# The last load of wo split in two, and the second half of K*e moved behind the next head's row maximum, in a one-core forward and backward decode kernel

## The chip, the cores and the metric

The kernel runs on one core of one Trainium2 chip. Its time is the device time of one execution in microseconds (us). The core has TensorE (PE; its weight loads are listed apart as PEld), VectorE (DVE), ScalarE (ACT) and GpSimd (POOL); SyncE (SP) issues most loads and computes nothing. Each engine works through its own list of instructions in order; what one makes for another is handed over by a semaphore, and an instruction that waits holds up all that stands behind it on its engine. Sixteen DMA engines move data between HBM and the on-chip memory.

## The reference

Both outputs and all gradients of a block with one query per batch element are computed (B = 2, H = 32 heads, 4096 cached keys, head size 128, D = 640, Dff = 1728):

```python
q = layernorm(x) @ wq                       # per head: [B, H, 1, 128]
scores = einsum("bhqd,bhkd->bhqk", q, k_cache) * 128 ** -0.5
p = softmax(scores);  o = einsum("bhqk,bhkd->bhqd", p, v_cache)
h  = x + o @ wo
h2 = h + relu(layernorm(h) @ w1) @ w2
out, vjp = jax.vjp(f, x, k_cache, v_cache, wq, wo, w1, w2);  return out, *vjp(grad_out)
```

The caches hold 64 heads (batch element and head) of 4096 x 128 numbers, 1 MiB each for K and for V. The gradients for K and V are as large again.

## The kernel before

The 64 heads pass the core twice. The **first pass** (`p1_iter`, L459 to L584) reads K and V of each head, forms the scores s = K q, e = exp(s - max), and three sums over the keys: V^T e, V^T (K*e) (a 128 x 128 matrix) and the column sums of K*e. The **second pass** (`p2_iter`, `p2_tail`) reads V once more (tile W), forms dP = V go and writes gK and gV. Between them stands the middle of each batch element (`middle_gen`): attention output times wo, layer norm, MLP forward and backward, and then the products of wo with the gradient, row by row (`go_group`), which the second pass of a head waits for. These rows, and those of w1 and w2 before, are dot products on DVE of 640 numbers (`ttr`, L656; called "row products" below); a counter `slot` says how many of them may be issued in each step of an iteration.

**One iteration of the first pass** is a software pipeline over three heads: head i is scored, K*e is formed for head i-1, and the sums over V are made for head i-2. It runs in steps k = 0 to 7, each ended by a `yield`, at which the loop at L1219 slips in steps of the second pass, the middle's work and the issue of loads. Per iteration:

- k0: PE transposes two quarters of K (T, L433), copied to SBUF by ACT (L438).
- k1: PE spreads the row maximum of head i-1 over all partitions (MX, L512), DVE reduces it to nb (L514); PE does the first 8 of 32 matmuls of V^T(K*e) for head i-2 (`m_part`, L467).
- k2: ACT makes ep = exp (L521); third transposed quarter; scores of quarter 0 (`pair_matvec`, L446).
- k3: `m_part(2)`; DVE forms the first half of K*e for head i-1 (`pk_half(0)`, L474); scores of quarter 1; last transposed quarter, copied by DVE up to i = 32 (L436) and by ACT afterwards.
- k4: `u_part` (column sums), `m_part(3)`, scores of quarter 2, `m_part(4)`.
- k5: second half of K*e (`pk_half(1)`), and K's buffer is given back; `m_part(5)`, `m_part(6)`; at its end `a_heads` (four heads of the attention output times wo, 20 matmuls at L603, added up by DVE at L605).
- k6: `m_part(7)`, scores of quarter 3, and DVE's row maximum rmax (L568), which the next iteration's MX waits for.
- k7: V's buffer is given back.

K*e has three buffers (`pk`, L481), so that its second half for one head goes where the first half for the head before was, which PE must have read (`u_part`, `m_part(3)`).

**Loads.** K, V, W and w2 share 13 tiles of 1 MiB (`ld`). All loads are issued by SP in one fixed order (`queue`, L1107 to L1123); a load waits until the tile that it goes to was given back and read, and those behind it wait too. In iteration i the next K and V are issued as soon as `pk_half(1)` and `m_part(7)` have let go of theirs. V of heads 26 to 31 stays for the second pass. wo comes in four quarters of 1280 KB, placed in the list at i = 10, 15, 29 and 33, and w1 at 35 (`W_AT`).

**Stages.** Iterations 0 to 33 are the first batch element alone, with w2's row products on DVE in iterations 12 to 29. Iterations 34 to 40 carry the first middle (w1's 15 row products, then wo's). From iteration 41 on (`P2_AT`) one head of the second pass runs beside every two iterations: in odd iterations PE also transposes W, in even ones DVE forms most of gK and gV (L830, written to HBM from POOL's queue). After iteration 65 the second pass runs alone. "Iteration 34" and the like mean i in `p1_iter(i)` below; its end is dated by its row maximum at L568.

Of the kernel before, what the change touches and what calls it, by code (L numbers as in the profile page):

```python
# [15 lines left out]
def kernel(  # L16
# [38 lines left out]
    OG = 4  # L55
# [285 lines left out]
    def pair_rows(dst, src, hs, bs):  # L341
# [6 lines left out]
        for c in range(2):  # L348
            rows = slice(64 * c, 64 * c + 64)
            for par in range(2):  # L350
                nc.vector.tensor_copy(out=dst[rows, bs, hs, par, c].rearrange("p b h -> p h b"), in_=t[rows, par, :, :])

    def load_weights(k):
        if k < 4:
            hs = slice(k * H // 4, (k + 1) * H // 4)
            nc.sync.dma_start(out=wo_t[:, hs, :], in_=wo_r[:, hs, :])
        elif k == 4:
            nc.sync.dma_start(out=w1_t[:], in_=B_w1.rearrange("(c p) f -> p c f", p=128))

    FP = 6  # L360
# [64 lines left out]
    def pair_transpose(nat, g, dve=False, busy=0):  # L425


        t_ps = pst([128, GT // 2, 128], FP32, "tps", "t_ps")
        warm(t_ps[:].rearrange("p j k -> p (j k)"), nat, g, busy)
        natf = nat[:].bitcast(FP32)  # L430
        for j in range(GT // 2):
            cc = (g * GT) // 2 + j
            nc.tensor.transpose(t_ps[:, j, :], natf[:, 2 * cc:2 * cc + 2, :].rearrange("p c k -> p (c k)"), ident_f[:])  # L433
        t_sb = mats.tile([128, GT // 2, 128], FP32, tag="XT", bufs=4, name="t_sb")
        if dve:
            nc.vector.tensor_copy(out=t_sb[:], in_=t_ps[:])  # L436
        else:
            nc.scalar.copy(out=t_sb[:], in_=t_ps[:])  # L438
        return t_sb

    def pair_matvec(dst, t_sb, g, vecs):
        v = t_sb[:].bitcast(BF16).rearrange("p j (k two) -> p j k two", two=2)
        for j in range(GT // 2):
            sc = g * GT + 2 * j
            for par in range(2):
                nc.tensor.matmul(dst[:, sc:sc + 2], lhsT=v[:, j, :, par], rhs=vecs[:, par, :],  # L446
                                 start=(par == 0), stop=(par == 1))
# [11 lines left out]
    def p1_iter(i, dve_group, busy):  # L459
# [5 lines left out]
        def m_part(k):  # L465
            for sc in range(4 * k, 4 * k + 4):
                nc.tensor.matmul(r["m"][:, 0:129], lhsT=r["V"][:, sc, :],  # L467
                                 rhs=r["pk"][sc // HALF][:, sc % HALF, 0:129],
                                 start=(sc == 0), stop=(sc == NSC - 1))

        def pk_half(k):

            sl = slice(k * HALF, (k + 1) * HALF)
            nc.vector.tensor_tensor(  # L474
                out=p["pk"][k][:, :, 0:128].rearrange("p s (a two) -> p s a two", two=2),
                in0=p["K"][:, sl, :].rearrange("p s (a two) -> p s a two", two=2),
                in1=p["ep"][:, sl, None, :].to_broadcast([128, HALF, 64, 2]), op=ALU.mult)
# [51 lines left out]
            c["s"] = c["bank"][:, 0:NSC]  # L529
            pair_matvec(c["s"], c.pop("KT0"), 0, q)  # L530
        yield
        if r is not None:
            m_part(2)
        if p is not None:
            pk_half(0)
        if c is not None:
            pair_matvec(c["s"], c.pop("KT1"), 1, q)
            c["KT3"] = pair_transpose(c["K"], 3, dve_group)
        yield
        if r is not None:  # L540
            u_part()
            m_part(3)
        if c is not None:
            pair_matvec(c["s"], c.pop("KT2"), 2, q)
        if r is not None:
            m_part(4)
        if p is not None and hp % OG == OG - 1:

            totp = p["bank"][:, 256:256 + OG]
# [2 lines left out]
        if p is not None:  # L552
            pk_tile(1)
            if hp % OG == OG - 1:
                nc.vector.reciprocal(out=rt[:, bp, hp + 1 - OG:hp + 1], in_=totp)
            (nc.gpsimd if i < P2_AT else nc.vector).tensor_copy(out=P_bf[:, p_slot[(bp, hp)], :], in_=ep[:, :, 0])
            pk_half(1)
            give(p["K"], "g" if i == P2_AT else None)
        if r is not None:
            m_part(5)  # L560
            m_part(6)
        yield
        if r is not None:
            m_part(7)
        if c is not None:
            pair_matvec(c["s"], c.pop("KT3"), 3, q)
            rmax = small.tile([128, 1], BF16, tag="rmax", bufs=2, name="rmax")
            nc.vector.reduce_max(out=rmax[:], in_=c["s"], axis=AX.X)  # L568
            c["rmax"] = rmax
        yield  # L570
        if r is not None:
            br, hr = pairs[i - 2]
# [35 lines left out]
    def a_heads(i):  # L608

        if a_next[0] < o_next[0]:  # L610
            a_group()
        if o_next[0] < NP1 // OG and i >= o_next[0] * OG + OG + 2:
            b, g = divmod(o_next[0], H // OG)
            if b > 0 or i >= O_AT[g * OG * 4 // H]:
                o_group()

    def u_out(b, u4):
# [41 lines left out]
    slot = [99]  # L659
# [445 lines left out]


    queue = []  # L1107
    W_AT = (10, 15, 29, 33, 35)
    O_AT = (14, 19, 30, 32)
    W2_AT = (8, 13, 18)  # L1110
    for n, (ii, jj) in enumerate(plan):
        if ii is not None:
# [45 lines left out]
    for n, (i, j) in enumerate(plan):  # L1158
        all_go = all(("go", B - 1, h) in done for h in range(H))
        if i is None and plan[n - 1][0] is not None:  # L1160
            pkp.release()
            big1 = tc.alloc_tile_pool(name="big1", bufs=1)
            for _ in range(2):
                more_home("ld", big1)
            share(ld=KEPT[1] + 4, g=5)
        if all_go and not late[0]:
            wop.release()
            big3 = tc.alloc_tile_pool(name="big3", bufs=1, side="right")
            for tag in ("ld", "g", "g", "q", "q", "q"):
                more_home(tag, big3)  # L1170
        late[0] = all_go
        more = int(late[0])
        if fin is not None and not bg2 and not bg3:
            share(ld=8 + 3 * more, g=7 + 3 * more)
        elif fin is not None and j >= H:
            held = sum(bh in kept for bh in turns[j + 1:])
            share(ld=5 + held + more, g=5 + 2 * more, f=3, q=2 + 3 * more)
        while g2 is not None:
            p2_step()
        open_tail = [k for k in S2 if "T3" in S2[k]]  # L1180
        if j is not None:
            if j < NP1:
                bg_until(("go", *turns[j]))
            g2 = p2_iter(j, i is None and j < H) if j < NP1 else p2_tail(NP1 - 1)
        elif open_tail:
            g2 = p2_tail(open_tail[0])
        if i is None and ("w1", 1) in done and fin is None:
            wts.release()
            fin = tc.alloc_tile_pool(name="fin", bufs=1)
            big2 = tc.alloc_tile_pool(name="big2", bufs=1)  # L1190
            more_home("f", big2)
            banks.update(sps=[2, 3], o=[4, 5, 6])
            bg2.append(("fin", fin_gen(fin)))
            bg3.append(("gx", gx_gen(fin)))
        if i == 12:
            bg.append(("ga", ga_gen()))
        if i == H + 2:
            banks["bc"].insert(0, banks["sps"].pop(0))
        elif i == P2_AT:
            banks["bc"].remove(7)  # L1200
            banks["sps"].insert(0, banks["bc"][0])
            banks["bc"] = [7]
        rate = RATES[0 if i is not None and i <= H + 1 else 1 if j is None and i < P2_AT else
                     2 if i is not None else 3 if j <= H else 4]
        if i is None:
            spread[0] = 2
            at_k[0] = 1
            k = 0
            while g2 is not None:
                p2_step()  # L1210
                pump()
                slot[0] = int(k in ((1, 3, 5) if j <= H else (1, 4)))
                k += 1
                bg_step(0, rate)
                bg_step(1, RATE2 * (0.4 if spreading[0] else 1.0))
                bg_step(2, RATE3)
            continue
        at = LIGHT if j is None else HEAVY_TAIL if open_tail else HEAVY
        for k, _ in enumerate(p1_iter(i, i < H + 1, 0)):  # L1219
            for _ in range(at.get(k, 0)):  # L1220
                if g2 is not None:
                    p2_step()
            if k == 5:
                a_heads(i)
            pump()

            spread[0] = 1 if i < P2_AT else 2
            at_k[0] = k
            if i >= P2_AT:
                slot[0] = int(k == 6 or (k == 1 and j is None))  # L1230
            elif i > H + 1:
                slot[0] = {1: 2, 3: 1, 4: 1, 6: 1}.get(k, 0)
            else:
                slot[0] = int(k in (1, 6))
            bg_step(0, rate)
            bg_step(1, 0.0)
        if i is not None and i in (H + 1, NP1 + 1):
            bg.append((f"m{i // H - 1}", middle_gen(i // H - 1)))
# [41 lines left out]
```

## Time and profile before

Three timed executions took 897.49, 898.05 and 899.12 us (median 898.05). The profiled execution took 896.79 us, of which the span of the core's instructions, which all views of the trace cover, is 895.0 us.

| what | profile before |
|---|---|
| PE, DVE, ACT, POOL busy | 745.7, 686.9, 482.9, 197.3 us of 895.0 |
| moved by DMA | 361.84 MB, mean 404 GB/s |
| half of K*e on DVE (L474) | 128 x 1221 ns |
| row product (L656), with its read of the sum | 816 + 81 ns |
| half of gK or gV on DVE (L830) | 1223 and 1143 ns |
| row maximum (L568), nb (L514) on DVE | 193 and 290 ns |
| last quarter's copy on DVE (L436) | 680 ns |
| SP waiting for K*e (L474) before a load | 124.7 us in 20 waits |
| SP waiting for PE's transposes (L433) | 257.7 us in 47 waits |

Times are counted from the span's start. DMA share is the busy share of the 16 DMA engines (1.0 is all of them, and records can overlap to slightly more). "PEclk" is the clock that PE was granted, as a share of the full one. A number in brackets in a timeline is the idle time of the engine before an instruction, with what ended it.

### The profile page before, as it was taken

Reading aid. Unit: us, or ns where it says so; the run is one execution under the profiler, and the core shown is the slowest. Engines: PE = TensorE matmul, PEld = TensorE weight load, DVE = VectorE, ACT = ScalarE, POOL = GpSimd, SP = SyncE. Lnnn points to the kernel's source line nnn. Section 1 sums busy time; section 2 is a strip of 40 time slices with the busy share of each in tenths; the row PEclk is TensorE's granted clock in tenths of the full one; section 3 lists DMA queues with packets and bytes.
Section 4 is the critical chain, followed back from the end, with each engine's and each line's share of the span. In section 5 each row is a group of like instructions: output and inputs, shape, how many; then the busy total and the mean of one; then the engine's idle time right before and its main releaser. Section 6 shows DMA issues by size and latency. Waiting matters only on the chain.

```text
span 895.0 us, 24702 instructions
## 1 busy us (share of the span) xinstructions
PE 745.7 (83%) x10145; PEld 622.3 (70%) x10145; DVE 686.9 (77%) x1283; ACT 482.9 (54%) x1236; POOL 197.3 (22%) x347
## 2 busy tenths in 40 slices
PE   4999899999998999797967786778797897978593
PEld 4887788888887888686857675566666665665452
DVE  2666788866888897686768896679986579998854
ACT  1344344443555655464535777776665765657462
POOL 1344444442310000000011241122221111111211
PEclk9999999998999999799885555555755755555555
DMA  9999999999989999999999999999999999999996
GB/s 379 419 412 402 411 407 419 409 412 411 358 300 365 423 422 424 423 421 424 401 398 381 418 418 415 390 419 391 416 420 404 426 424 425 424 424 426 423 411 277
DMA packets 56288, 361.84 MB, mean 404 GB/s; under 512 B 5680, under 2 KB 11888, under 8 KB 15472
## 3 DMA queue, kind: packets, MB, share of 16 engines
q1 hardware_dynamic: 34520, 211.13, 58.2%
q0 software_dynamic: 18432, 134.23, 36.1%
q10 hardware_dynamic: 3224, 14.92, 4.1%
q8 instruction: 80, 1.31, 0.6%
q14 instruction: 32, 0.26, 0.1%
HBM read 211.11 MB, written 149.13 MB: 403 GB/s over the span
## 4 chain that ended last, share of the span: by engine, by line
PE 37%; DMA 26%; DVE 21%; issue 7%; ACT 7%; SPq 0%; POOL 0%; ACTq 0%; POOLq 0%; DVEq 0%
PE t_ps L433 15%; DMA Vt<-in_A_v_cache_dram 11%; DMA out_dram<-gK 10%; PE m_ps L467 8%; DVE rows L656 5%; DVE gK L830 5%; DVE gV L830 5%; DMA out_dram<-gV 3%; DVE pk L474 3%; PE s_ps L446 3%; ACT gV L897 3%; PE u_ps L496 2%; PE o_ps L948 2%; PE dp_ps L446 2%; ACT t_sb L438 2%
## 5 line engine op out<-in xcount | busy, mean ns | idle before, releaser
L438 ACT COPY t_sb<-t_ps 128x512 f32<-128x512 f32 x479 | 271.8, 587 | 203.4 <-PE t_ps L433 200.4
L446 PEld LDWEIGHTS <-t_sb 128*128 128x128 bf16 x4096 | 180.8, 103 | 61.4 <-ACT t_sb L438 30.0
L433 PE MATMUL t_ps<-ident_f,Wt 128*128 128x128 f32 x832 | 202.5, 396 | 0.8 <-ACT t_sb L438 0.8
L474 DVE TENSOR_TENSOR pk<-Kt,ep 128x2048 bf16<-128x2048 bf16 x128 | 156.2, 1221 | 43.6 <-PE m_ps L467 20.1
L467 PE MATMUL m_ps<-pk,Vt 128*128 128x129 bf16 x2048 | 173.6, 223 | 15.2 <-DMA Vt<-in_A_v_cache_dram 14.7
L830 DVE TENSOR_TENSOR gK<-rb,gsp 128x2048 bf16<-128x2048 bf16 x128 | 153.0, 1223 | 13.7 <-DMA out_dram<-gV 12.1
L433 PEld LDWEIGHTS t_ps<-ident_f,Wt 128*128 128x128 f32 x832 | 141.6, 206 | 30.7 <-issue 22.3
L433 PE MATMUL t_ps<-ident_f,Kt 128*128 128x128 f32 x1024 | 154.2, 285 | 4.2 <-DMA Kt<-in_A_k_cache_dram 4.1
L467 PEld LDWEIGHTS <-Vt 128*128 128x128 bf16 x2048 | 125.4, 99 | 46.1 <-issue 28.7
L830 DVE TENSOR_TENSOR gV<-rb,pp 128x2048 bf16<-128x2048 bf16 (+1 forms) x128 | 143.3, 1143 | 12.3 <-DMA out_dram<-gK 9.8
L484 POOL COPY pk<-ep 128x16 bf16<-128x16 bf16 x80 | 85.2, 1067 | 152.7 <-ACT ep L521 72.4
L433 PEld LDWEIGHTS t_ps<-ident_f,Kt 128*128 128x128 f32 x1024 | 113.5, 145 | 5.1 <-PE s_ps L446 2.7
L446 PE MATMUL dp_ps<-gom,t_sb 128*128 128x2 bf16 x2048 | 96.4, 168 | 19.9 <-ACT t_sb L438 19.5
L898 POOL DMA_DIRECT2D out_dram<-gV x64 | 34.2, 534 | 314.2 <-DVE nb L514 114.2
L446 PE MATMUL s_ps<-gom,t_sb 128*128 128x2 bf16 x2048 | 87.5, 164 | 1.3 <-DVE t_sb L436 1.3
L849 POOL DMA_DIRECT2D out_dram<-gK x64 | 34.0, 532 | 210.4 <-DVE gK L830 164.0
L580 ACT CAST MT<-m_ps 128x128 bf16<-128x128 f32 x64 | 17.1, 267 | 104.9 <-PE m_ps L467 104.7
L954 ACT CAST ot<-o_ps 128x512 bf16<-128x512 f32 (+3 forms) x152 | 67.5, 491 | 3.1 <-PE o_ps L948 1.9
L656 DVE CUSTOM_DVE_ANT_0 rows<-wo_t,rows 128x640 bf16<-128x640 bf16 x64 | 52.4, 819 | 0.2
L841 DVE SCALAR_TENSOR_TENSOR gsp<-dp_ps,negdot,P_bf 128x64 bf16<-128x64 f32 x64 | 17.8, 279 | 42.5 <-PE dp_ps L446 42.4
L870 ACT ACTIVATE rb<-dp_ps,rt 128x256 bf16<-128x256 f32 x64 | 30.3, 473 | 36.9 <-PE dp_ps L865 35.7
L656 DVE CUSTOM_DVE_ANT_0 rows<-wqs,gqr 128x1024 bf16<-128x1024 bf16 x40 | 48.7, 1219 | 0.2
(194 smaller groups left out, 758.8 us busy)
## 6 DMA issues: line engine op xcount, KB each, us to landing
Kt<-in_A_k_cache_dram SPq DMA_DIRECT2D x64, 1024.0 KB, 16.9
Vt<-in_A_v_cache_dram SPq DMA_DIRECT2D x64, 1024.0 KB, 18.1
out_dram<-gV POOLq DMA_DIRECT2D x64, 1024.0 KB, 12.1
out_dram<-gK POOLq DMA_DIRECT2D x64, 1024.0 KB, 13.0
Wt<-in_A_v_cache_dram SPq DMA_DIRECT2D x52, 1024.0 KB, 11.7
out_dram<-ot ACTq DMA_DIRECT2D x6, 960.0 KB, 6.6
wq_t<-in_A_wq_dram SPq DMA_DIRECT2D x5, 1024.0 KB, 9.8
wo_t<-in_A_wo_dram SPq DMA_DIRECT2D x4, 1280.0 KB
```

The costliest lines, as they stand in the source:

```text
L433: nc.tensor.transpose(t_ps[:, j, :], natf[:, 2 * cc:2 * cc + 2, :].rearrange("p c k -> p (c k)"), ident_f[:])
L438: nc.scalar.copy(out=t_sb[:], in_=t_ps[:])
L446: nc.tensor.matmul(dst[:, sc:sc + 2], lhsT=v[:, j, :, par], rhs=vecs[:, par, :], start=(par == 0), stop=(par == 1))
L467: nc.tensor.matmul(r["m"][:, 0:129], lhsT=r["V"][:, sc, :], rhs=r["pk"][sc // HALF][:, sc % HALF, 0:129], start=(sc == 0), stop=(sc == NSC ...
L474: nc.vector.tensor_tensor(out=p["pk"][k][:, :, 0:128].rearrange("p s (a two) -> p s a two", two=2), in0=p["K"][:, sl, :].rearrange("p s (a ...
L484: nc.gpsimd.tensor_copy(out=col, in_=e)
L656: nc.vector.tensor_tensor_reduce(out=junk[0:kc, 0:width], in0=in0, in1=in1, scale=1.0, scalar=0.0, op0=ALU.mult, op1=ALU.add, accum_out=acc)
L830: nc.vector.tensor_tensor(out=pairs_view(dst[:, sl, :]), in0=row.rearrange("p (a two) -> p a two", two=2)[:, None, :, :].to_broadcast([128 ...
L849: nc.gpsimd.dma_start(out=natural(out_2, bp, hp), in_=gK[:])
L870: nc.scalar.activation(out=rb[:], in_=bank[:, 128:384], func=ACT.Copy, scale=rt[:, b, h:h + 1])
L898: nc.gpsimd.dma_start(out=natural(out_3, b, h), in_=gV[:])
L954: nc.scalar.copy(out=ot[0:P, k, n0:n0 + nn], in_=o_ps[0:P, 0:nn])
```

## The change

wo's last quarter is loaded as two parts of four heads, the second one iteration later, in front of w1's load. On PE, `m_part(2)` moves behind the scores of quarter 1, `m_part(3)` and `m_part(4)` ahead of `u_part`, and `m_part(7)` behind the scores of quarter 3. On DVE, `pk_half(1)` moves from step 5 to step 6, behind the row maximum of head i; K's buffer is given back there too. In iterations 34 to 40 the row products' slots move from steps 1, 3, 4, 6 (2, 1, 1, 1) to steps 1, 3, 4 (2, 2, 1). The order of ACT's and POOL's instructions is the same as before.

```diff
+    WO_PARTS = (0, H // 4, H // 2, 3 * H // 4, H - OG, H)
+
     def load_weights(k):
-        if k < 4:
-            hs = slice(k * H // 4, (k + 1) * H // 4)
+        if k < len(WO_PARTS) - 1:
+            hs = slice(WO_PARTS[k], WO_PARTS[k + 1])
             nc.sync.dma_start(out=wo_t[:, hs, :], in_=wo_r[:, hs, :])
-        elif k == 4:
+        else:
             nc.sync.dma_start(out=w1_t[:], in_=B_w1.rearrange("(c p) f -> p c f", p=128))
...
         yield
-        if r is not None:
-            m_part(2)
         if p is not None:
             pk_half(0)
         if c is not None:
             pair_matvec(c["s"], c.pop("KT1"), 1, q)
+        if r is not None:
+            m_part(2)
+        if c is not None:
             c["KT3"] = pair_transpose(c["K"], 3, dve_group)
         yield
         if r is not None:
+            m_part(3)
+            m_part(4)
             u_part()
-            m_part(3)
         if c is not None:
             pair_matvec(c["s"], c.pop("KT2"), 2, q)
-        if r is not None:
-            m_part(4)
...
             (nc.gpsimd if i < P2_AT else nc.vector).tensor_copy(out=P_bf[:, p_slot[(bp, hp)], :], in_=ep[:, :, 0])
-            pk_half(1)
-            give(p["K"], "g" if i == P2_AT else None)
         if r is not None:
             m_part(5)
             m_part(6)
         yield
-        if r is not None:
-            m_part(7)
         if c is not None:
             pair_matvec(c["s"], c.pop("KT3"), 3, q)
...
             c["rmax"] = rmax
+        if p is not None:
+            pk_half(1)
+            give(p["K"], "g" if i == P2_AT else None)
+        if r is not None:
+            m_part(7)
         yield
...
-            if b > 0 or i >= O_AT[g * OG * 4 // H]:
+            if b > 0 or i >= O_AT[g]:
                 o_group()
...
-    W_AT = (10, 15, 29, 33, 35)
-    O_AT = (14, 19, 30, 32)
+    W_AT = (10, 15, 29, 33, 34, 35)
+    O_AT = (14, 14, 19, 19, 30, 30, 32, 33)
...
-                slot[0] = {1: 2, 3: 1, 4: 1, 6: 1}.get(k, 0)
+                slot[0] = {1: 2, 3: 2, 4: 1}.get(k, 0)
```

As the lists of the two programs show, DVE in iterations 34 to 47 gets this order (pk is a half of K*e, ttr a row product, gkv a half of gK or gV, the rest small operations or named above):

```
36 before  small nb pk ttr ttr rt pk rmax
   after   pk small nb pk ttr ttr ttr rt rmax
37 before  ttr nb ttr ttr pk ttr ttr pk rmax
   after   pk nb ttr ttr pk ttr ttr ttr rmax
39 before  ttr nb ttr ttr small pk small pk small rmax
   after   pk nb ttr ttr small pk small rmax
40 before  nb ttr ttr small pk small pk rmax
   after   pk nb ttr ttr small pk small rmax
46 before  ttr gkv nb gsp ttr pk gkv Pbf pk small rmax
   after   pk ttr gkv nb gsp ttr pk gkv Pbf small rmax
47 before  gkv ttr nb pk Pbf pk gkv small rmax
   after   pk gkv ttr nb pk Pbf gkv small rmax
```

On PE the 20 matmuls of L603 for heads 28 to 31 stand where they stood, in iteration 34 ahead of MX and of the first `m_part`; their first weight load now waits for the second part of wo's last quarter.

## The prediction

> **What bounds the kernel now.** I read the page's slices first, then the stages by windows, then the waits of SP, and last the timelines of PE and DVE where a stage is not limited by DMA.
>
> ```profile
> PE   4999899999998999797967786778797897978593
> PEclk9999999998999999799885555555755755555555
> DMA  9999999999989999999999999999999999999996
> GB/s 379 419 412 402 411 407 419 409 412 411 358 300 365 423 422 424 423 421 424 401 398 381 418 418 415 390 419 391 416 420 404 426 424 425 424 424 426 423 411 277
> ```
>
> A slice is 22.4 us. The DMA engines are full nearly everywhere, at 402 to 419 GB/s while only reads run and about 423 when writes are mixed in; slices 10 to 12 stand out with 358, 300 and 365 GB/s. The stages:
>
> ```profile
> 0.00:224.00 224.00, 203.55 (x3494) 179.42 (x3495) 155.53 (x328) 86.09 (x252) 84.89 (x122) 0.98 1.01 408
> 224.00:252.00 28.00, 25.57 (x461) 22.34 (x459) 24.31 (x64) 13.79 (x39) 7.99 (x13) 1.00 0.92 358
> 252.00:282.00 30.00, 28.29 (x484) 25.12 (x483) 24.19 (x57) 18.28 (x49) 3.08 (x7) 1.00 0.83 300
> 282.00:343.00 61.00, 56.12 (x973) 49.78 (x971) 52.58 (x106) 36.41 (x100) 5.22 (x12) 1.00 1.01 423
> 432.00:464.00 32.00, 27.88 (x479) 24.36 (x477) 26.18 (x49) 18.07 (x50) 4.63 (x9) 1.00 0.99 389
> ```
>
> The columns are length, busy PE, PEld, DVE, ACT, POOL, clock, DMA share, GB/s. Up to 224 us DMA is full (1.01): no engine's order can shorten that stage, except through when it ends. From 224 to 282 us DMA waits for buffers: against 423 GB/s, 28 x (1 - 358/423) + 30 x (1 - 300/423) = 4.3 + 8.7 = 13.0 us are lost there. This hole is what the change can win or enlarge. It ends where the last loads that DMA idles for are issued:
>
> ```profile
> 280.24 0.33 SPq L454 DMA_DIRECT2D Vt<-in_A_v_cache_dram  x1
> 280.97 0.33 SPq L454 DMA_DIRECT2D Kt<-in_A_k_cache_dram  x1
> 281.91 0.33 SPq L454 DMA_DIRECT2D Vt<-in_A_v_cache_dram  x1
> ```
>
> Afterwards the queue never runs dry until 432 us, so what is lost or won up to these three lines is what the end shows, plus 432 to 464 us (389 GB/s).
>
> **The entry into the hole: wo's split.**
>
> ```profile
> 208.90 1.06 PE L433 MATMUL t_ps<-ident_f,Kt 128*128 128x128 f32 x8 [0.71 <-DMA Kt<-in_A_k_cache_dram]
> 209.80 0.64 PE L603 MATMUL a_ps<-OFc,wo_t 128*128 128x1 bf16 x20
> 210.31 0.22 PE L512 MATMUL s_ps<-neg_ident,rmax 128*128 128x128 bf16 x1
> 211.29 1.05 PE L467 MATMUL m_ps<-pk,Vt 128*128 128x129 bf16 x8 [0.77 <-DMA Vt<-in_A_v_cache_dram]
> ```
>
> In iteration 34 PE waits 0.71 us for K of head 34 and 0.77 us for V of head 32. Half a quarter of wo is 0.655 MB, at 411 GB/s 1.6 us: with only the first half ahead of them both land 1.6 us earlier, and both waits go. But the second half of wo, now last of the same bytes, lands when V did, at 211.2, and the 20 matmuls at L603 need it ahead of MX and of the first eight `m_part` matmuls. So these start at 211.2 + 0.5 (from 209.80 to 210.31) + 0.1 = 211.9 instead of 211.29. I take **+0.6 us**; the bounds are -1.6 (all of the earlier landing kept) and +0.6.
>
> **The middle, iterations 34 to 40.** The sums of DVE's work are the same per iteration, only pk changes sides of rmax.
> - 35 and 36: before, rmax at 219.09 is followed at once by small operations of the layer norm and nb starts at 220.08. Now pk (1.22) stands ahead of them; nb and the norm's result come about 1.5 us later. PE had spare time there (DVE idled 1.44 us before the rmax of 225.93), so I let +0.6 reach rmax 35, and +0.1 rmax 36. Bounds 0 and +1.5.
> - 34 and 35: `m_part(7)` leaves the way to rmax: 4 matmuls, 0.24 us each time (one such group starts at 222.55 and what follows it at 222.79). I take -0.3 of -0.48, since part of it falls where DVE sets the pace.
> - 37: DVE is full in 230 to 248 us; a pk (1.15 from start to start) stands in for a row product (0.87): **+0.3**.
> - 39: one row product of w1's last five (0.61 + 0.08) has moved to 36: **-0.6**.
> - 40: before, DVE idles 1.36 us for nb at 253.34; pk fits in: **-1.15**.
>
> With the split: 0.6 + 0.7 - 0.3 + 0.3 - 0.6 - 1.15 = **-0.45** at the end of iteration 40.
>
> **Beside the second pass.** An odd and the next even iteration:
>
> ```profile
> 289.73 0.18 DVE L568 TENSOR_REDUCE rmax<-s_ps 128x1 bf16<-128x32 f32 x1
> 291.71 0.28 DVE L514 TENSOR_REDUCE nb<-s_ps 128x1 f32<-128x128 f32 x1
> 293.21 0.66 PE L433 MATMUL t_ps<-ident_f,Vt 128*128 128x128 f32 x4 [0.41 <-ACT t_sb L438]
> 294.97 1.22 DVE L474 TENSOR_TENSOR pk<-Kt,ep 128x2048 bf16<-128x2048 bf16 x1 [1.19 <-PE m_ps L467]
> 297.57 0.19 DVE L568 TENSOR_REDUCE rmax<-s_ps 128x1 bf16<-128x32 f32 x1 [0.24 <-PE s_ps L446]
> 303.05 1.21 DVE L474 TENSOR_TENSOR pk<-Kt,ep 128x2048 bf16<-128x2048 bf16 x1
> 304.45 0.19 DVE L568 TENSOR_REDUCE rmax<-s_ps 128x1 bf16<-128x32 f32 x1
> ```
>
> From the even rmax to nb DVE is full (2.0 us); from nb over ACT's exp and copies to PE's transposes, on which PE waits 0.41 us, PE sets the pace up to the odd rmax (5.86); from there DVE is full to the next even rmax (6.88). The pair takes 14.72. The odd pk at 294.97 lies in a stretch where DVE idles anyway; moved behind the odd rmax it enters the DVE-bound even half, which hands its own pk on to the next odd one, ahead of nb. So the first piece grows by 1.15 to 1.25, the second shrinks by 0.24 (`m_part(7)`), the third keeps its work: **+1.0 us per pair**. For 41 to 44 that is +2.0; in 43 and 44 some small operations of `go_group` (0.75, 0.5 and a 0.87 row product) shift one iteration on, out of the PE-bound 43, for which I take -1.5: **+0.5**, bounds -1.0 and +2.0. From 282 to 432 us the same +1.0 is hidden by the full DMA; the cover is thin only at first.
>
> **Buffers.** K's tile is now free 1.35 us (0.1 + 1.22) after rmax. It was free at rmax in even iterations, and 1.9 us ahead of it in 43 (280.2 against 282.09). In program order the load of 280.24 now takes W's tile, released by PE at 280.95, the next K's, at 282.1 + 1.35 = 283.4. The three issues move by about +0.7, +2.5 and +1.5; I take **+1.5**, bounds 0 (the queue covers it) and +2.5.
>
> **432 to 464 us** holds one and a half pairs; DMA is nearly full, so I take half of +1.5: **+0.7**, bounds 0 and +1.5.
>
> **The first 224 us: 0.** Covered by DMA. Were DMA not the bound, the loop over nb, exp, pk, copy and rmax would lose a pk (5.22 to about 4.9 where no row product runs, PE then being the bound: 33 x 0.3 = 10 us won), while with two row products per iteration it would grow, since nothing covers the wait for the last scores any more (by some 0.4). SP's order of loads is not moved past anything but the second part of wo; it is one more issue, 0.4 us on a queue that issues 165.
>
> **Sum:** -0.45 + 0.5 + 1.5 + 0.7 = +2.25, say +2.2: span 897.2. The profiled execution was 1.8 us longer than its span and 1.26 us under the median, so against the median: 898.05 + 2.2 = **900.2 us**.
>
> **Rivals.**
>
> 1. *The clock stays full in iteration 34, and the earlier rmax pays: faster.* PE's clock falls behind a poorly filled stretch:
>
> ```profile
> 207.83:211.25 3.42, 1.98 (x41) 1.76 (x37) 1.93 (x10) 1.70 (x6) 0.08 (x1) 1.00 1.00 411
> 211.25:218.07 6.82, 6.78 (x69) 5.87 (x70) 3.17 (x11) 1.27 (x4) 0.76 (x2) 0.50 1.01 410
> ```
>
> 1.98 of 3.42 us busy (0.58), then 6.8 us at half clock, which cost about 3.4 us of PE work. A first pass that comes later to iteration 34 (row products ahead of nb in 13 to 28) or stalls that fall into two stretches would avoid it: -3.4. With the buffers' term at 0 as well: 2.2 - 3.4 - 1.5 = -2.7, **895.3 us**. Against it: wo's second part makes one wait of over 2 us out of two short ones. Chance 0.33, for both signs hang on 0.58 or a little more.
>
> The Trainium skill, TensorE: Matmul & The Clock Gate, "What's actually happening", says that the clock falls after at least one idle window of about 3.4 us; by that rule a wait of 2 us would not lower it, and the sum would be this rival's first step, 2.2 - 3.4 = -1.2. The trace does not agree: 0.58 busy was enough here, so I go by the trace.
>
> 2. *Nothing to be seen.* If the queue covers the later buffers and the end of the first pass, -0.45 + 0.5 are left: **898.1 us**. For it: 423 GB/s from 282 us on. Against it: the three issues above end an idle DMA. Chance 0.20.
>
> 3. *Slower by much more.* If the +1.0 is not hidden in the ten pairs from 43 to 64: 2.2 - 0.7 + 10 - 0.5 = +11, **909 us**. Against it: DMA at 1.01 from 282 to 432 us. Chance 0.09.
>
> **How the numbers follow.** The forecast has 0.38. Two executions differ by 0.2% (1.8 us) without a cause, so that is what I call no change. Faster 0.33 (rival 1), same 0.20 (rival 2), slower 0.47 (forecast and rival 3). The gaining bounds together are -1.6 - 3.4 - 0.3 - 0.6 - 1.15 = -7 (891), the losing ones 0.6 + 1.5 + 0.3 + 2.0 + 2.5 + 1.5 - 1.75 = +6.6 (904.7); I take 891 to 905, which leaves out rival 3 and little else. For the forecast alone it is 898.5 to 904.
>
> **What would show it.** Right: the first `m_part` of iteration 34 behind L603 at about 212 us; rmax to rmax over two iterations near 15.7 from 45 on, with DVE waiting for the odd rmax; loads of K issued 1.3 us behind rmax; the hole as deep as before and ending 1 to 2 us later. Wrong: clock 1.00 from 211 to 218 us; GB/s over 380 in slices 10 to 12; a DMA share clearly under 1 before 200 us, or under 1 from 290 to 430.

## The result and the profile after

Eleven executions of the changed kernel took 904.55 us in the median (899.72 to 907.8), beside 898.23 us (897.0 to 900.53, 11 runs) for the kernel before. The ratio is 1.0059, 95% interval [1.0043, 1.0074]: slower by 0.6%, some 5.3 us. The forecast was 900.2 us with a range of 891 to 905. The profiled execution took 904.55 us, 902.8 of it span (before: 895.0).

The slices of the page of the changed kernel, each 22.6 us:

```profile
PEclk9999999999899999998995555555755756555555
DMA  9999999999788999999999999999999999999996
GB/s 378 419 411 405 409 404 420 408 414 407 310 331 304 391 424 424 423 423 421 418 355 365 416 415 420 408 396 394 418 422 400 426 425 425 424 424 426 424 420 286
```

The first ten slices are as before. Slices 10 to 12 now have 310, 331 and 304 GB/s (before 358, 300, 365), slice 13 has 391, and there is a deeper second dip at 355 and 365 (before 398 and 381), where the first pass ends. The same stages as were shown of the kernel before, by windows:

```profile
0.00:224.00 224.00, 202.19 (x3522) 178.86 (x3523) 150.63 (x327) 86.10 (x252) 48.68 (x122) 0.98 1.01 408
224.00:252.00 28.00, 26.14 (x399) 22.37 (x397) 23.24 (x58) 13.44 (x37) 6.75 (x12) 0.88 0.80 309
252.00:282.00 30.00, 26.82 (x441) 23.07 (x440) 23.38 (x53) 17.00 (x47) 3.29 (x9) 0.97 0.84 312
282.00:343.00 61.00, 53.93 (x938) 48.30 (x935) 48.01 (x99) 34.08 (x94) 4.93 (x10) 0.98 1.00 397
432.00:464.00 32.00, 26.76 (x441) 23.19 (x442) 24.36 (x55) 16.23 (x45) 3.91 (x6) 0.95 0.97 390
```

The line that matters is the fourth: 397 GB/s where the kernel before moved 423, in the very stage in which the prediction let a full DMA hide DVE's longer work. DVE is busy for 48.0 us there instead of 52.6, so it did less, not more: it waited. PE's clock is not full in the second to fifth line (0.88, 0.97, 0.98, 0.95), where it was in the kernel before.

Adding up the bytes of the trace's DMA packets in order of time gives the time at which each kernel has moved a given amount; the difference is how far one is behind the other:

| moved | time, before | after is behind by | what lies there |
|---|---|---|---|
| 90 MB | 220.7 us | +0.3 us | end of the stage that DMA sets |
| 110 MB | 281.2 us | +2.9 us | end of the hole |
| 120 MB | 304.8 us | +6.3 us | first pairs beside the second pass |
| 170 MB | 423.0 us | +6.3 us | DMA full |
| 180 MB | 447.9 us | +5.5 us | |
| 200 MB | 498.7 us | +8.8 us | end of the first pass |

After that the difference stays (+8.7 at 340 MB; the spans differ by 7.8, the medians by 6.3). So the bytes fall behind in three stretches: by 2.9 us in the hole, by 3.4 us from 284 to 311 us, and by about 2.5 us net at the end of the first pass. The bytes show a late load only when its data were due (a load of K took 16.9 us from issue to landing in the median, in the kernel before). Counted by the issue of the loads, as the prediction counts, the first two are for the most part one loss: the last load of the hole is issued 5.5 us later, as is shown below. The prediction had 1.55 us for that, 0 for what comes behind it and 0.7 for the end of the first pass.

**What makes the loads late.** From the even row maximum of iteration 46 to the odd one of 47 the changed kernel's timelines of DVE, ACT and PE show (start, duration, engine, line; in brackets the idle time before, and what ended it):

```profile
308.97 0.19 DVE L566 TENSOR_REDUCE rmax<-s_ps 128x1 bf16<-128x32 f32 x1
309.07 1.21 DVE L476 TENSOR_TENSOR pk<-Kt,ep 128x2048 bf16<-128x2048 bf16 x1
310.20 1.22 DVE L833 TENSOR_TENSOR gK<-rb,gsp 128x2048 bf16<-128x2048 bf16 x1
311.34 0.82 DVE L659 CUSTOM_DVE_ANT_0 rows<-wo_t,rows 128x640 bf16<-128x640 bf16 x1
312.08 0.28 DVE L516 TENSOR_REDUCE nb<-s_ps 128x1 f32<-128x128 f32 x1
312.40 0.31 ACT L523 ACTIVATE ep<-s_ps,nb 128x64 bf16<-128x64 f32 x1 [1.23 <-DVE nb L516]
313.58 0.66 PE L435 MATMUL t_ps<-ident_f,Vt 128*128 128x128 f32 x4 [1.57 <-ACT t_sb L440]
318.07 0.16 DVE L608 TENSOR_TENSOR asum<-asum,a_ps 128x5 f32<-128x5 f32 x1 [2.78 <-PE a_ps L606]
318.27 0.19 DVE L566 TENSOR_REDUCE rmax<-s_ps 128x1 bf16<-128x32 f32 x1
```

nb starts 3.1 us behind the row maximum, where it started 2.0 us behind it before; the half of K*e at 309.07 is what came in between. ACT waits 1.23 us for nb, PE 1.57 us (0.41 before) for ACT's copy, and then DVE waits 2.78 us for PE: the time that the half used to fill. Two iterations, odd and even, measured between even row maxima:

| iterations | 41+42 | 43+44 | 45+46 | 47+48 | 49+50 |
|---|---|---|---|---|---|
| before, us | 14.59 | 16.44 | 14.71 | 15.98 | 14.53 |
| after, us | 16.16 | 17.67 | 16.41 | 15.98 | 16.00 |

Then the loads follow the rhythm. Timelines of DVE and SP in the changed kernel, about the ends of iterations 43 and 44:

```profile
285.60 0.19 DVE L566 TENSOR_REDUCE rmax<-s_ps 128x1 bf16<-128x32 f32 x1
285.71 1.22 DVE L476 TENSOR_TENSOR pk<-Kt,ep 128x2048 bf16<-128x2048 bf16 x1
286.95 0.33 SPq L456 DMA_DIRECT2D Kt<-in_A_k_cache_dram  x1
287.37 0.39 SPq L456 DMA_DIRECT2D Vt<-in_A_v_cache_dram  x1
292.56 0.18 DVE L566 TENSOR_REDUCE rmax<-s_ps 128x1 bf16<-128x32 f32 x1
293.90 0.33 SPq L456 DMA_DIRECT2D Kt<-in_A_k_cache_dram  x1
```

Each K goes out the moment that the half behind the row maximum is done, 1.34 us behind that maximum, and V right behind it. The last load of the hole is issued at 287.37 instead of 281.91, 5.5 us later: 3.5 us because the row maximum of 43 is later, 2 us because K's buffer is.

Of the 3.5 us, 1.6 are there at the row maximum of 42. The other 1.9 come in iteration 43, where PE ran at half clock from 280.42 to 283.83 us. The same window of the two profiles, the kernel before first:

```profile
280.00:290.00 10.00, 9.17 (x167) 8.13 (x164) 9.18 (x23) 5.75 (x17) 0.53 (x1) 1.00 1.01 422
280.00:290.00 10.00, 10.00 (x169) 8.28 (x167) 5.73 (x17) 3.85 (x12) 0.49 (x1) 0.83 0.98 339
```

In the window of 3.42 us ahead of the half clock, from 277.00 us on, PE was busy for 1.79 us (0.52): nb came 3.2 us behind the row maximum of 42, and PE waited 1.63 us for ACT's copy behind it.

### The profile page after: what moved, and what is told of

It reads as the page before. It is cut to its first block, busy times and chain, and to the rows that moved or that the text cites. A ratio compares the mean times of both kernels' runs of the same rounds, so it can differ in the third digit from the quotient of the medians.

```text
span 902.8 us, 24677 instructions
## 1 busy us (share of the span) xinstructions
PE 745.1 (83%) x10145; PEld 620.5 (69%) x10145; DVE 682.2 (76%) x1283; ACT 481.7 (53%) x1236; POOL 163.0 (18%) x347
## 3 DMA queue, kind: packets, MB, share of 16 engines
q8 instruction: 80, 1.31, 0.6%
## 4 chain that ended last, share of the span: by engine, by line
PE 32%; DVE 21%; DMA 20%; issue 7%; ACT 7%; POOL 0%; ACTq 0%; POOLq 0%; SPq 0%; DVEq 0%
PE t_ps L435 13%; DMA out_dram<-gK 11%; PE m_ps L469 6%; DMA Vt<-in_A_v_cache_dram 6%; DVE gK L833 6%; DVE rows L659 5%; DVE pk L476 4%; DVE gV L833 3%; DMA out_dram<-gV 3%; PE s_ps L448 3%; ACT gV L900 2%; ACT t_sb L440 2%; PE dp_ps L448 2%; PE o_ps L951 2%; PE u_ps L498 2%
## 5 line engine op out<-in xcount | busy, mean ns | idle before, releaser
L448 PEld LDWEIGHTS <-t_sb 128*128 128x128 bf16 x4096 | 169.8, 103 | 93.7 <-ACT t_sb L440 41.2
L469 PE MATMUL m_ps<-pk,Vt 128*128 128x129 bf16 x2048 | 175.7, 224 | 11.0 <-DMA Vt<-in_A_v_cache_dram 9.8
L435 PE MATMUL t_ps<-ident_f,Kt 128*128 128x128 f32 x1024 | 150.0, 281 | 4.9 <-DMA Kt<-in_A_k_cache_dram 4.7
L469 PEld LDWEIGHTS <-Vt 128*128 128x128 bf16 x2048 | 130.7, 100 | 14.5 <-DMA Vt<-in_A_v_cache_dram 12.1
L448 PE MATMUL s_ps<-gom,t_sb 128*128 128x2 bf16 x2048 | 80.0, 164 | 5.9 <-ACT t_sb L440 4.4
L486 POOL COPY pk<-ep 128x16 bf16<-128x16 bf16 x80 | 49.1, 622 | 191.0 <-ACT ep L523 155.1
L659 DVE CUSTOM_DVE_ANT_0 rows<-wqs,gqr 128x1024 bf16<-128x1024 bf16 x40 | 48.7, 1219 | 0.2
L659 DVE CUSTOM_DVE_ANT_0 rows<-w_t,rows 128x640 bf16<-128x640 bf16 (+2 forms) x58 | 45.7, 787 | 3.9 <-ACT rows L637 3.0
```

The costliest lines, as they stand in the source:

```text
L469: nc.tensor.matmul(r["m"][:, 0:129], lhsT=r["V"][:, sc, :], rhs=r["pk"][sc // HALF][:, sc % HALF, 0:129], start=(sc == 0), stop=(sc == NSC ...
L486: nc.gpsimd.tensor_copy(out=col, in_=e)
L659: nc.vector.tensor_tensor_reduce(out=junk[0:kc, 0:width], in0=in0, in1=in1, scale=1.0, scalar=0.0, op0=ALU.mult, op1=ALU.add, accum_out=acc)
```

## The experiments

Four theories were set against each other. **A**: the half of K*e that moves behind the odd row maximum enters the stretch in which DVE sets the pace, and DMA does not cover it at first. **B**: the half clock and the later buffers in iterations 34 to 40 did it. **C**: the new order on PE did. **K**, added later: K's buffer, given back later, costs by itself. Every kernel was timed beside the kernel before on the same chip (897.89, 897.75 and 897.75 us in the median of the three groups). "GB/s" is that of the window 282 to 311 us of one profile (before: 423, changed kernel: 369).

| kernel | us, median | ratio, 95% interval | GB/s |
|---|---|---|---|
| after_pk_ahead_p2 | 895.91 | 0.9989 [0.9974, 1.0004] | 421 |
| before_pk_behind_p2 | 904.43 | 1.0082 [1.0060, 1.0105] | 344 |
| before_split_only | 898.33 | 1.0010 [0.9996, 1.0025] | 416 |
| before_pe_order_only | 897.93 | 1.0000 [0.9986, 1.0014] | 423 |
| before_pk_behind_odd | 902.75 | 1.0059 [1.0038, 1.0080] | 390 |
| before_pk_behind_even | 897.64 | 1.0003 [0.9989, 1.0017] | 413 |
| before_extra_row_odd | 899.22 | 1.0024 [1.0012, 1.0036] | 423 |
| after_pk_behind_even | 897.66 | 1.0008 [0.9997, 1.0020] | 421 |
| before_late_k_odd | 900.21 | 1.0029 [1.0015, 1.0042] | 400 |
| before_extra_and_late_k_odd | 900.83 | 1.0035 [1.0018, 1.0053] | 394 |
| before_pk_behind_first | 897.52 | 0.9998 [0.9985, 1.0010] | 424 |
| after_pk_ahead_p2_whole_quarter | 897.76 | 0.9993 [0.9981, 1.0004] | 423 |

### Which part of the change

The changed kernel, with the half (and K's return) in its old place from iteration 41 on:

```diff
+            if i >= P2_AT:
+                pk_half(1)
+                give(p["K"], "g" if i == P2_AT else None)
...
-        if p is not None:
+        if p is not None and not (i >= P2_AT):
             pk_half(1)
```

> The changed kernel, but from iteration 41 on (P2_AT) the second half of K*e is formed in step 5 again, ahead of the row maximum. Theory A (the move costs a K*e per pair of iterations beside the second pass, and DMA did not cover it): the pairs go from 15.7-16.4 us back to about 14.7-15.3, the stage 282-343 us back to 423 GB/s, ratio to before 0.998 to 1.002 (about 5 us under the changed kernel's 1.006). Theory B (the loss is the half clock and the buffers in iterations 34 to 40): no more than 1 us better than the changed kernel, ratio 1.005 to 1.007.

0.9989, and 421 GB/s from 282 to 311 us. Nothing of the loss is left, though all the rest of the change is in.

The reverse, the kernel before with only that move:

```diff
-            pk_half(1)
-            give(p["K"], "g" if i == P2_AT else None)
+            if i < P2_AT:
+                pk_half(1)
+                give(p["K"], "g" if i == P2_AT else None)
...
             c["rmax"] = rmax
+        if p is not None and not (i < P2_AT):
+            pk_half(1)
+            give(p["K"], "g" if i == P2_AT else None)
```

> The kernel before with one edit: from iteration 41 on the second half of K*e is formed behind the row maximum. Theory A: slower by 4 to 7 us, ratio 1.004 to 1.008, with GB/s under 410 in 282-343 us. Theory B: ratio 0.999 to 1.002.

1.0082: this part alone costs at least as much as the whole. The loss sits where it does in the changed kernel: 344 GB/s from 282 to 311 us, 9.9 us behind at 120 MB, 12.2 at 200 MB. A is right so far, and B can't be the main cause, as iterations 34 to 40 are those of the kernel before here.

The split of wo alone (the `WO_PARTS`, `W_AT` and `O_AT` lines of the diff), and PE's order alone (`m_part(2)`, `(3)`, `(4)` and `(7)` moved as in the diff):

> The kernel before with wo's last quarter split in two, nothing else. The prediction's term: first m_part of iteration 34 at 211.9 instead of 211.3 us, +0.6 us if the clock falls as before. If the waits before it become too short for the clock to fall (rival 1), iteration 34 ends 2 to 3 us earlier and the ratio is 0.997 to 0.999. Theory B would have the clock fall in iteration 36 instead and the ratio 1.002 to 1.004.

> The kernel before with PE's order of the changed one (m_part 2, 3, 4, 7 moved), K*e ahead of the row maximum as before. Prediction: m_part(7) leaves the way to the row maximum, 0.24 us per PE-bound iteration, ratio 0.998 to 1.000. If PE's order is what costs (rival C), ratio 1.003 or more.

1.0010 and 1.0000, neither told from no change. C is out. The split may cost up to 0.0025 or nothing.

The move up to iteration 40 alone (shown), and the changed kernel with neither the move from 41 on nor the split:

```diff
-            pk_half(1)
-            give(p["K"], "g" if i == P2_AT else None)
+            if i >= P2_AT:
+                pk_half(1)
+                give(p["K"], "g" if i == P2_AT else None)
...
             c["rmax"] = rmax
+        if p is not None and not (i >= P2_AT):
+            pk_half(1)
+            give(p["K"], "g" if i == P2_AT else None)
```

> The kernel before with the second half of K*e behind the row maximum up to iteration 40 only. The prediction gave 0 to the first 224 us (covered by DMA) and -0.85 us to iterations 35 to 40 and the buffers there; if so the ratio is 0.998 to 1.000. If the later second half and the later K buffer cost at the entry into the hole, 1.001 to 1.003. A half clock that falls in another iteration moves a profile by up to 3 us without a cause in the edit.

> The changed kernel with the second half of K*e ahead of the row maximum again from iteration 41 on, and with wo's last quarter in one load. If the split costs what its own run showed (1.0010 [0.9996, 1.0025]), this is 0.001 below that kernel with the split (0.9989): ratio 0.997 to 0.999. If the split is worth nothing either way, 0.998 to 1.000. If what was gained there hangs on the split, 1.000.

0.9998 and 0.9993. Without its part from iteration 41 on, no form of the change was shown to be worth anything; no version tried beats the kernel before by more than its interval.

### Which half of a pair

The move in odd or in even iterations from 41 on only (the old place under `if i < P2_AT or i % 2 == 0:`, else the new one; and with `i % 2 == 1`), and the changed kernel with the half back in its old place in odd iterations:

> The kernel before with the second half of K*e behind the row maximum in odd iterations from 41 on, alone. Theory A by pieces of a pair: even rmax to nb 2.0, nb to odd rmax 5.9, odd rmax to even rmax 6.9 + 1.15: pair 15.9 us instead of 14.7, ratio 1.004 to 1.009. Theory K (what costs is that K's buffer is free later, not DVE's order): the odd move frees it 3 us later and costs too, ratio 1.003 or more.

> The same in even iterations from 42 on, alone. Theory A: the K*e leaves the DVE-bound piece (6.9 - 1.15) and enters the piece to the next nb, also DVE-bound (2.0 + 1.15): pair 14.7 us as before, ratio 0.998 to 1.002. Theory K: the buffer is free 1.3 us later in each pair, ratio 1.001 to 1.004.

> The changed kernel with the second half of K*e ahead of the row maximum in odd iterations from 41 on, behind it in all others. Theory A: as good as the one with it ahead from 41 on (ratio 0.9989), 0.997 to 1.001. Theory K: 1.001 to 1.004.

Alone, only the odd half costs: 1.0059 against 1.0003. In the even iterations the half merely changes places inside DVE's full stretch (a pair takes 14.95 us in the mean of 45 to 52, in the kernel before 15.06; with the odd move 16.19). With it back in its place in odd iterations only, the changed kernel is at 1.0008; that run was expected to tell whether the even move is free beside the other edits, and it is, to about 0.2%. Whether the even half adds to the odd one stays open: both together, in the kernel before, cost 1.0082, with an interval that overlaps that of the odd move. In that profile PE is at half clock from 281.15 to 287.98 us and again from 301.63 to 305.05, and a pair takes 17.08 us; in that of the odd move alone there is no half clock in this stretch, and iteration 43 is as long as in the kernel before.

### Why the odd half costs: DVE's stretch or K's buffer

The moved half does two things at once, so each was imitated without moving it. First DVE's part: a row product whose result nothing uses, behind the odd row maximum.

```diff
             c["rmax"] = rmax
+            if i >= P2_AT and i % 2 == 1:
+                ttr(wo_t[:, 0, 0:636], wo_t[:, 1, 0:636], rows3[:, 0, 638:640].bitcast(FP32), 636)
```

> The kernel before with one more row product on DVE (0.9 us, its result is used by nothing) right behind the row maximum of odd iterations from 41 on. No buffer is let go of later by it except through the longer chain. Theory A: pair 15.6 us, about 0.8 of the loss of the odd move, ratio 1.003 to 1.007. Theory K: ratio 0.999 to 1.002.

1.0024, less than expected: a pair grows by 0.86 us (15.92 in the mean of 45 to 52) as it should, but 282 to 311 us keep their 423 GB/s. What the longer stretch costs, it costs in the hole: the pair 41+42 lies in it, and its 0.86 us reach the last load of the hole, which is 1.7 us later (0.9 of them were there at iteration 40, ahead of the first added product). Behind the hole the pairs go on growing, and the bytes fall hardly further behind (+1.8 us at 110 and at 120 MB, +2.0 at 170) until the end of the first pass (+2.6 at 200). Then the buffer's part: K given back in odd iterations only behind a copy of one column, just ahead of the next nb.

```diff
+            if i - 1 > P2_AT and (i - 1) % 2 == 1:
+                nc.vector.tensor_copy(out=rows3[:, 0, 638:639], in_=r["K"][:, 31, 127:128])
+                give(r["K"])
             nc.tensor.matmul(mx, lhsT=p["rmax"][:].to_broadcast([128, 128]), rhs=neg_ident[:], start=True, stop=True)
...
-            give(p["K"], "g" if i == P2_AT else None)
+            if not (i > P2_AT and i % 2 == 1):
+                give(p["K"], "g" if i == P2_AT else None)
```

> The kernel before; in the odd iterations 43 to 63 K's buffer is given back only behind a copy of one column that DVE makes just ahead of the next nb, about 2 us behind the odd row maximum (the change gives it back 1.35 us behind it, the kernel before about 2 us ahead of it). No half of K*e moves; DVE gets 11 copies of about 0.1 us. Theory A (only DVE's longer stretch costs): ratio 1.000, 282 to 343 us at 420 GB/s or more, and at equal bytes no more than 0.5 us behind the kernel before. Theory K (the later loads cost too: 1.0059 for the move in odd iterations less 1.0024 for an added row product of the same place): ratio 1.002 to 1.004, and the delay arises between 282 and 311 us.

1.0029, with DVE's rhythm nearly unchanged (15.26 us a pair; 45+46 take 15.35 instead of 14.71, the three pairs after them are within 0.1 us of before). The copy came later than was planned: K is free 3.1 us behind the odd row maximum of 43, 1.8 us later than in the change. The timelines of SP and DVE in this kernel show how the loss arises:

```profile
283.93 0.33 SPq L454 DMA_DIRECT2D Kt<-in_A_k_cache_dram  x1
284.12 0.19 DVE L572 TENSOR_REDUCE rmax<-s_ps 128x1 bf16<-128x32 f32 x1 [0.28 <-PE s_ps L446]
287.07 0.15 DVE L513 COPY rows<-Kt 128x1 bf16<-128x1 bf16 x1
287.24 0.33 SPq L454 DMA_DIRECT2D Vt<-in_A_v_cache_dram  x1
```

The V load behind the K of 283.93 is to go into the K tile that is held back, and is issued as the copy ends, 3.3 us behind K; in the kernel before 0.94 us lie between those two. Reads run short, as the windows of this kernel show:

```profile
283.00:288.00 5.00, 5.00 (x105) 4.50 (x102) 4.18 (x15) 2.51 (x9) 0.53 (x1) 1.00 1.01 372
288.00:293.00 5.00, 4.09 (x64) 3.56 (x61) 5.00 (x9) 2.68 (x9) 0.00 (x0) 1.00 0.99 344
293.00:300.00 7.00, 6.59 (x117) 5.87 (x115) 4.89 (x10) 4.74 (x13) 0.78 (x2) 1.00 1.01 425
```

So, in this profile, one late buffer at the moment when the queue has just caught up costs about 1.5 us (from +2.0 us behind at 110 MB to +3.5 at 120 MB), although nothing computes longer. K is right as well as A: here A acts on the iterations in the hole, K on the loads that end it.

Both imitations together, K's return now 1.1 us behind the odd row maximum:

```diff
             c["rmax"] = rmax
+            if i >= P2_AT and i % 2 == 1:
+                ttr(wo_t[:, 0, 0:636], wo_t[:, 1, 0:636], rows3[:, 0, 638:640].bitcast(FP32), 636)
+        if p is not None and i > P2_AT and i % 2 == 1:
+            nc.vector.tensor_copy(out=rows3[:, 0, 638:639], in_=p["K"][:, 31, 127:128])
+            give(p["K"])
```

> The kernel before with both imitations of the moved half in odd iterations: from 41 on a row product of 636 numbers behind the odd row maximum, whose result nothing uses, and in 43 to 63 a copy of one column of K behind that, after which K's buffer is given back (1.1 to 1.2 us behind the odd row maximum). Both halves of K*e stay where they were. Theory A with K: the two costs add up to that of the move, ratio 1.005 to 1.007. Theory A alone: as with the row product only, 1.002 to 1.003. If the move costs through something else (the order in which PE gets K*e, for one), it is 1.002 to 1.003 too, and the run above is 1.000.

1.0035 [1.0018, 1.0053]: less than the sum of the two, and below the 1.0059 [1.0038, 1.0080] of the real move, though the intervals overlap. The pair (16.14 us) and the 394 GB/s from 282 to 311 us are close to those of the real move (16.19 and 390). Each imitation falls short of what it stands for (0.9 us of DVE's time for 1.15 to 1.25, a return at 1.1 us for 1.35), so the remainder may be size alone; whether something else adds to it stays open, and so does the exact share of each. How much later than in the profile of the kernel before each step comes, in us:

| kernel | row maximum of 40 | of 43 | last load of the hole | 120 MB moved |
|---|---|---|---|---|
| before_extra_row_odd | +0.9 | +1.7 | +1.7 | +1.8 |
| before_late_k_odd | +2.0 | +2.0 | +5.3 (the K ahead of it +3.0) | +3.5 |
| before_extra_and_late_k_odd | +0.5 | +1.3 | +3.1 | +3.2 |
| before_pk_behind_odd | +0.8 | +2.5 | +4.5 | +4.5 |
| changed kernel | 0.0 | +3.5 | +5.5 | +6.3 |

In the first four rows the first column is there without an edit, since these kernels differ from iteration 41 on. From iteration 40 to the last load both imitations lose 2.6 us and the odd move 3.7: 1.7 instead of 0.9 in the iterations, 2.0 instead of 1.8 at K's buffer. Except where K was held back longest, the bytes at 120 MB are behind by as much as the last load is, to within 0.8 us. The profiled run took 904.49 us against a median of 900.83 for both imitations, and 900.49 against 902.75 for the odd move, so the profiles serve to place the losses and not to rank these two.

## Why the prediction was right, and where its size was off

**The sign and the mechanism held.** It forecast slower, through the second half of K*e behind the odd row maximum and through K's later buffer, and the single parts show just these two. The even move alone, PE's order and the split were worth nothing that could be told, as their small terms said. The size was too small: 904.55 us lies just inside the range and above the 898.5 to 904 that were given for the forecast alone.

**The term that was mis-sized** is that for iterations 41 to 44, "**+0.5**, bounds -1.0 and +2.0". The row maximum of 43, behind which the last loads of the hole go out, came **3.5 us** later, that of 44 2.8 us. The pair 41+42 grew by 1.57 us instead of 1.0, and iteration 43 by 1.9. The -1.5 for `go_group`'s operations, which were to leave 43, did not show. The half clock in 43 was in no term; by an estimate its 3.41 us can have cost 1.7 us of PE's work at most, so that 43 would have been no shorter without it. With K's buffer, 2 us for the 1.5 taken, the last load of the hole was 5.5 us late instead of 1.55.

"From 282 to 432 us the same +1.0 is hidden by the full DMA; the cover is thin only at first" held nearly. The bytes are +6.3 us behind at 120 MB and at 170 MB, while the row maxima go on from +4.5 us in iteration 46 to +7.8 in 52. Between the last load (+5.5) and 120 MB (+6.3) 0.8 us are lost for which there was no price. The 397 GB/s of that stage are for the most part the late loads of the hole, seen when their data were due, and not a second loss.

**The pair** was to take 15.7 us and to grow by 1.0; it took 16.4 and 16.0 in 45 to 48. Over 45 to 52 it grew from 15.06 to 16.30, by 1.24: the size was nearly right, and the three pieces were named rightly.

**The rest of the hole**: -0.45 up to iteration 40. Its row maximum was at +0.02 us; a profile alone doesn't settle a difference of that size there, as the last section shows.

**The end of the first pass**: +0.7 taken, about +2.5 net in this profile (windows 451 to 480 and 480 to 510 us have 371 and 374 GB/s, before 400 and 401). The upper bound was 1.5. How much of it belongs to the change stays open: between 180 and 200 MB the kernel with the half in its old place from 41 on lost 0.2 us with the split and 3.3 us without it, and neither is slower than the kernel before.

**Two slips of the working**: the gaining bounds leave out the -1.0 of iterations 41 to 44, with which the range would start at 890 us, and SP issues 180 loads of K, V and W alone, not 165 in all. Nothing hangs on either.

**The entry** came as written, and one thing did not. The timeline of PE in the changed kernel:

```profile
211.32 0.65 PE L606 MATMUL a_ps<-OFc,wo_t 128*128 128x1 bf16 x20 [0.88 <-DMA wo_t<-in_A_wo_dram]
211.83 0.22 PE L514 MATMUL s_ps<-neg_ident,rmax 128*128 128x128 bf16 x1
211.89 0.63 PE L469 MATMUL m_ps<-pk,Vt 128*128 128x129 bf16 x8
```

The matmuls of wo wait for its second part, and `m_part` starts at 211.89 us (predicted 211.9). But one wait of 0.88 us took the place of two, not one of over 2 us, and the clock stayed full: the marker that was to speak for the first rival. It didn't pay, since the half clock came two iterations later, as windows of the changed kernel on PE's clock show:

```profile
218.98:222.39 3.41, 2.21 (x40) 1.57 (x37) 2.70 (x10) 1.38 (x4) 1.62 (x3) 1.00 1.02 412
222.39:225.80 3.41, 3.41 (x96) 3.38 (x94) 1.44 (x4) 0.33 (x2) 0.00 (x0) 1.00 0.96 401
225.80:232.63 6.83, 6.22 (x62) 5.17 (x60) 3.90 (x10) 3.40 (x8) 1.30 (x1) 0.50 0.93 375
```

Iteration 34 takes 7.26 us instead of 10.87, iteration 36 10.05 instead of 6.77: won and given back, +0.02 us at the end of iteration 40.

**The other markers**: K's loads 1.34 us behind the row maximum (1.3 written), DVE waiting for the odd one (2.78 us), GB/s under 380 in slices 10 to 12: all as written. The hole did not end 1 to 2 us later, but 2.9 by bytes and 5.5 by its last load. One marker was badly chosen: a DMA share under 1 from 290 to 430 us. The share stayed at 1.00 from 282 to 343 us, and the loss was in GB/s. Rival 3 (ten pairs unhidden, 909 us) had the pairs' growth come through in full; it did so up to the end of the hole, and behind it hardly.

## What to carry to other kernels

A full DMA covers longer iterations only once it no longer waits for loads. Look at what lets the last load go that it waits for, and up to there count every longer iteration and every later release as lost in full; behind it pairs longer by 0.9 us cost next to nothing here. Date a loss by the issue of the loads: here the bytes showed it up to some 20 us later. An operation that fills another engine's wait costs nothing where it stands; before it is moved, mark which stretches of the iteration its engine sets, since an equal sum of work per iteration says nothing of that. A buffer given back a microsecond later is a change of its own, and should be tried apart from the work that moved with it.

## What the runs showed of the hardware

**The half clock moves from run to run.** Iterations up to 40 have the same instructions in the kernel before and in the six variants of it that differ from 41 on. In the profile of before PE's half clock lies in iteration 34 (10.87 us, iteration 36 6.77); in that of the kernel with the late K it comes in 36 (7.47 and 8.53 us). In the six profiles the row maximum of iteration 40 lies 0.5 to 2.4 us later than in that of before, with no edit behind it, so a single profile can't judge a term of that size in the hole. What sets it off isn't settled either: the prediction took it from one window 0.58 busy that was followed by the half clock at once; in the lines above a window of 2.21 of 3.41 us (0.65) was followed by a full one at full clock, and then by 6.8 us at half. In the same profile the window of 0.52 from 277.00 us was followed by it at once, and windows of 0.54 from 294.07 and from 311.14 us were not.

The Trainium skill, TensorE: Matmul & The Clock Gate, "What's actually happening", has the clock halved after at least one idle window of about 3.4 us. The length of the windows agrees with these traces (6.83 us is two of 3.41); an idle window was not needed here, since in the two windows ahead of the half clock of 225.80 us PE was busy for 0.65 and all of the time.

**Some half clocks go with an edit.** All four profiles with the second half of K*e behind the even row maximum from 41 on have a half clock that starts between 278 and 292 us (280.42, 281.15, 278.94 and 291.86); none of the ten others has one between 260 and 340 us. That the longer wait of PE for nb brings it on is likely, but not shown by a run of its own. Alone it cost nothing that could be told (1.0003 and 1.0008 with the even move).

**A DMA share near 1 is not full speed.** From 288 to 293 us the kernel with the late K shows a share of 0.99 at 344 GB/s, and the next window 1.01 at 425. The rate has to be read beside the share.

**A small copy on POOL took five times as long when it began behind a half of K*e on DVE.** In the kernel before a copy of 128x16 (L484) that began 0.03 us behind the half of 123.06 us took 1.31 us; in the changed kernel one that began at 120.90 us, 0.04 us ahead of a half, took 0.26. From 60 to 200 us the mean of these copies is 1172 ns before and 587 ns after, and POOL's busy time up to 224 us falls from 84.9 to 48.7 us with as many instructions. That stage is set by DMA in both kernels, so no time hangs on it.
